# GpSimd additions that wait for the VectorE sum ahead of them in a list schedule

## The chip, the core and the metric

The kernel runs on one core of a Trainium2 chip. The core has five engines that run side by side, each with its own in-order queue: TensorE (PE, with its weight loads shown as PEld), VectorE (DVE), ScalarE (ACT), GpSimd (POOL) and SyncE (SP, which here only issues DMAs). The metric is the device time of one execution in microseconds (us); three runs of the kernel as it was took 1032.78, 1033.08 and 1033.87 us, the median is 1033.08.

## The reference

Linear attention with exponential features, then a mixture of experts with Sinkhorn routing. Cut to what is computed (shapes of this case in comments):

```python
def phi(x):                                   # q, k, v: 8 x 8 x 576 x 64, w_phi: 64 x 128
    proj = np.einsum('bhsd,df->bhsf', x, w_phi)
    proj = proj - np.max(np.abs(proj), axis=-1, keepdims=True)
    return np.concatenate([np.exp(proj), np.exp(-proj)], axis=-1)
q_p, k_p = (phi(q), phi(k))
kv = np.einsum('bhsf,bhsd->bhfd', k_p, v)
...
x = attn_out.transpose(0, 2, 1, 3).reshape(B * S, H * D)      # 4608 x 512
P = np.exp(x @ w_gate - logits.max())                          # 4608 x 8 experts
for _ in range(8):
    P /= P.sum(1, keepdims=True) + 1e-09
    P /= P.sum(0, keepdims=True) + 1e-09
    P *= N / E
for e in range(E):
    h = np.maximum(x @ w1[e], 0.0)            # w1: 8 x 512 x 1024
    out += P[:, e:e + 1] * (h @ w2[e])        # w2: 8 x 1024 x 512
```

Every token goes through every expert, so the eight pairs of matrix products are most of the work.

## The kernel before

**Stages.** From 0 to about 202 us the attention runs, batch by batch, with expert 0's products filled in between. Then come the routing (`routing`) and experts 1 to 7. The tokens are cut into nine groups of 512 (`g`); groups 0 to 7 are taken in pairs, group 8 (the rests of all batches) alone. Per expert there are thus nine steps, two for each pair and one for group 8; the whole of an expert takes about 111 us in the profile.

**Seven products.** Experts 1 to 7 multiply 2 x 2 blocks with seven block products in place of eight (the Strassen-Winograd scheme), which needs sums and differences of blocks in bf16 and additions of results in f32. `up7` makes h = relu(x w1) and `down7` adds P times (h w2) to the result tile `acc` (4 x 512 f32 per group). The sums of blocks come from `sums_x` (of x, kept in DRAM and read back), `sums_up` (of w1), `sums_down` (of w2) and the loop over `fp` in `down7` (of h). All of them go through the helper `sub` (line 1205) and are VectorE `tensor_tensor` instructions of line 1209 with both operands and the result in SBUF. The profile names their tiles `hs` (h), `hx` (a tile that holds the sums and the two V buffers), `T`, `X`, `w` and `wx` (the two weight buffers).

**Who empties a PSUM bank.** There are eight banks of 512 f32. In `up7`, ScalarE copies a bank into another (`move`, line 1376) or into U (`keep`, line 1372) or applies the relu (line 1384), and VectorE adds a bank to U with saturation at 0, written to hs (`add`, line 1379). The products `x3` and `x4` share a bank: PE may start `x4` only when line 1379 has read `x3`. In `down7`, VectorE adds P times a bank to acc (`read`, line 1516), or ScalarE writes P times a bank into V (`read2`, line 1528, two instructions) and GpSimd adds V to acc (line 1531, 128 x 512 f32, both operands in SBUF). There are three such GpSimd additions per group and expert, and two V buffers.

**What sets the order.** Nothing is ordered by hand within a step except the list `ORDER` (line 1581), in which the parts are recorded. Each recorded operation (`Op`) has an engine, an estimated duration and its data dependencies. `Plan.schedule` (line 258) is a list schedule: again and again it takes the operation that can start first by its estimates, ties going to the one recorded first, and appends it to `done`. `Plan.run` (line 316) then issues the instructions in that order; each engine's queue is in order, and instructions of different engines wait for each other only where data requires it. One resource is modelled beside the engines: `Plan.port`, a time until which the operations marked `shared` may not start. VectorE's sums and all GpSimd operations but DMAs are `shared`; the drains of lines 1379 and 1516 are not. In the plan, then, a sum and a GpSimd addition never overlap. On the chip nothing orders them, since they touch different data.

**Other instructions in the queues concerned.** GpSimd's queue also issues the weight loads of the next expert (line 486, two DMAs per expert, behind an addition to group 4's acc). SP's queue reads the x sums back (line 1284) and stores the result (lines 1180 to 1194).

Of the kernel before, what the change touches and what calls it, by code (L numbers as in the profile page):

```python
# [17 lines left out]
class Buf:  # L18


    def __init__(self, ring):
        self.ring, self.t, self.slot, self.left, self.end = ring, None, None, 0, 0.0
        self.last = None
# [91 lines left out]

class Op:
    __slots__ = ("eng", "dur", "lat", "nbytes", "fn", "left", "ready", "users", "idx", "end",
                 "bufs", "deps", "shared", "turn", "unit", "stop", "tiled")

    def after(self, user):  # L120

# [77 lines left out]
class Plan:  # L199
# [3 lines left out]
    def __init__(self):  # L203
        self.last, self.readers = {}, {}
        self.ops = []
        self.prio = 0
        self.port = 0.0

    def op(self, eng, dur, lat, fn, r=(), w=(), takes=(), nbytes=0, shared=False):


        o = Op()
        o.eng, o.dur, o.lat, o.fn, o.nbytes = eng, dur, lat, fn, nbytes
        o.users, o.idx, o.end, o.ready = [], len(self.ops) + self.prio, None, 0.0
        o.shared, o.turn, o.unit, o.tiled = shared, False, 0, 0
        deps = {}
        for key in r:
            for d in self.last.get(key, ()):
                deps[id(d)] = d
        for key in w:  # L220
            for d in list(self.last.get(key, ())) + self.readers.get(key, []):
                deps[id(d)] = d
        bufs = list(takes)
        for key in list(r) + list(w):
            b = key[0] if isinstance(key, tuple) else key
            if isinstance(b, Buf):
                bufs.append(b)
        o.bufs = list({id(b): b for b in bufs}.values())
        for b in o.bufs:
            b.left += 1  # L230
        for key in r:
            self.readers.setdefault(key, []).append(o)
        for key in w:
            self.last[key] = [o]
            self.readers[key] = []
        o.deps = list(deps.values())
        o.left = len(o.deps)
        for d in o.deps:
            d.users.append(o)
        self.ops.append(o)  # L240
        return o

    def start(self, o, free):

        t = max(free, o.ready, self.port if o.shared else 0.0)
        need = {}
        for b in o.bufs:
            if b.slot is None:
                n = need[b.ring] = need.get(b.ring, 0) + 1
                at = b.ring.find(n)  # L250
                if at is None:
                    return None
                t = max(t, at)
            elif b.last is not None and b.last.eng != o.eng:
                t = max(t, b.last.end)
        return t

    def schedule(self):
        ready = {}
        free = {}  # L260
        links, clock = Links(), Clock()
        for o in self.ops:
            if o.left == 0:
                ready.setdefault(o.eng, []).append(o)
        done = []

        def finish(o):
            for b in o.bufs:
                if b.ring.psum:
                    b.last = o  # L270
                b.left -= 1
                b.end = max(b.end, o.end)
                if b.left == 0:
                    b.ring.give(b.end, b.slot)
            for u in o.users:
                u.left -= 1
                u.ready = max(u.ready, o.after(u))
                if u.left == 0:
                    ready.setdefault(u.eng, []).append(u)

        while len(done) < len(self.ops) or links.next():
            best = None
            for eng, rq in ready.items():
                f = free.get(eng, 0.0)
                if best is not None and f > best[0]:
                    continue
                for o in rq:
                    t = self.start(o, f)
                    if t is not None and (best is None or (t, o.idx) < best[:2]):
                        best = (t, o.idx, o)  # L290
            landed = links.next()
            if landed and (best is None or landed[0] <= best[0]):
                o = links.land(*landed)
                o.end = landed[0] + 1.0
                finish(o)
                continue
            assert best is not None, "no operation can start"
            at, _, o = best
            ready[o.eng].remove(o)
            for b in o.bufs:  # L300
                if b.slot is None:
                    b.slot = b.ring.take(at)
            dur = clock.takes(at, o.dur, o.tiled) if o.eng == "PE" else o.dur
            free[o.eng] = at + dur
            if o.shared:
                self.port = at + dur
            done.append(o)
            if o.nbytes:
                links.add(o, at)
            else:  # L310
                o.stop = at + dur
                o.end = o.stop + o.lat
                finish(o)
        return done

    def run(self, tc):
        done = self.schedule()
        with tc.manual_schedule():
            for o in done:
                o.fn()  # L320


@with_exitstack
def kernel(
# [158 lines left out]
    def load_w(e, r=()):  # L483
        w1, w2 = new("w1"), new("w2")
        for w, src in ((w1, moe_w1), (w2, moe_w2)):
            dma("POOL", 2 << 20, 280, lambda w=w, src=src: nc.gpsimd.dma_start(
                out=w(), in_=src[e].rearrange("(c p) f -> p c f", p=128)),
                r, [(w, i, j) for i in range(2) for j in range(2)])
        return w1, w2
# [569 lines left out]
    def stage_g(b):  # L1059
# [4 lines left out]
    at = [0]  # L1064
# [6 lines left out]
    order = (  # L1071
        "lraeaepqbwlqaqawwabwmqlltnrbppnwqbppmrmanbqaqmwwacmpnpbccpwbtcnmqnaqbclupunm"
        "taumquglcapalbcpnqqdcenmucugbblnapmrcqdutabnqpmunpbambccddnqplanmqmducpblttb"
        "augnaqlnrbdcampcadmqeutunqcppmdcaqtdqabpbbmlrqtdnpmuaqualbnagnacctbmqulupran"
        "tdpmtdqcmdnpdabdancpcabbqmpumqbcdgnappqunburqcbugmmnqdcdanumupqbnucmcpnmbddp"
        "bqmpncncubncmmgccg"
    )
# [25 lines left out]
    o = plan.op("X", 0.0, 0.0, swap, w=["late"])  # L1103
# [201 lines left out]
    def load_x(gs):  # L1305
        X = new_x()
        for n in (2, 3, 4):
            move_x(gs, n, False, X)
        return X
# [269 lines left out]


    ORDER = "X1 x10 w10 x11 X2 x20 y10 x21 Z1 y11 X3 w11 x30 x31 x40 x41 w20 Y1 w21 X4 Z2".split()
    END = "X1 p2 Y1 X2 Z1 p3 X3 Z2 X4 p0 p1".split()
    slots, wait = list(range(6)), []

    def take():
        z = [new(f"H{n}") for n in sorted(slots[:2])]
        del slots[:2]
        return z
# [16 lines left out]
    for e in range(1, E):  # L1605
        w1, w2 = load_w(e, ["late", ("acc", 4, 0, 0)] if e > 1 else ["late"])
        if e == 1:
            nextX = sums_x(pairs[0])
        A7 = sums_up(e, w1)
        B7 = sums_down(e, w2) if e > 1 else None  # L1610
        turn = [*pairs, (8,)] if e < E - 1 else [(8,), *pairs]
        for n, gs in enumerate(turn):
            X = nextX if e == 1 else load_x(gs)
            H = {g: [] for g in gs}
            for fp in range(len(gs)):
                hs = take()
                for i, z in enumerate(hs):
                    H[gs[min(i, len(gs) - 1)]].append(z)
                un = up7(A7, gs, fp, X, H, ["up0"])
                for o in ORDER:  # L1620
                    if len(o) == 3:
                        un[o[:2], int(o[2])]()
                    elif dn is not None:
                        dn[o]()
                if dn is not None:
                    dn["out"]()
                    slots.extend(dn["slots"])
                if e == 1 and fp == 0 and n + 1 < len(turn):
                    nextX = sums_x(turn[n + 1], [(H[gs[0]][0], 0, 1, 1)])
                if B7 is None and fp:  # L1630
                    B7 = sums_down(e, w2)
                if fp == len(gs) - 1:
                    wait += [(e, g, H[g], B7, w2, [z.ring.number for z in H[g]]) for g in gs]
                dn = next_down()
    last = next_down()
    for o in END:
        (dn if o[0] in "XYZ" else last)[o]()
# [32 lines left out]
```

## Time and profile before

| | |
|---|---|
| runs | 1032.78, 1033.08, 1033.87 us |
| the profiled execution's own time | 1032.32 us |
| its span, first to last instruction | 1030.2 us |
| PE busy | 1008.4 us (98%), 7944 matmuls |
| VectorE busy | 786.1 us (76%), 1707 instructions |
| ScalarE busy | 745.0 us (72%), 1594 |
| GpSimd busy | 380.0 us (37%), 418 |
| GpSimd additions, line 1531 | 186, 236.2 us in all, 1262 / 1268 / 1426 ns (min, median, max) |
| VectorE sums of 512 columns, `hx<-hx,hs` of line 1209 | 124, 409 / 416 / 1449 ns |
| VectorE sums of 1024 columns, `hx<-w` of line 1209 | 6, 691 / 1201 / 1722 ns |
| drains of line 1379 | 252, 673 / 690 / 694 ns |
| granted TensorE clock | 1.00 |

How to read it: the span is one profiled execution; the time of a run has about 2 us around it. Busy time is recorded time, and matmuls overlap in it: one of 256 columns is recorded with 0.27 us while the next starts 0.11 us later. The profile names instructions by line, engine, operation and tiles (out<-in), and puts idle time down to the instruction whose semaphore ended it. A line can be a helper's: all sums are line 1209, the products of the experts are lines 1317 and 1326. In a timeline, like instructions that follow each other are merged into one row with their number (x2) and their time from the first start to the last end.

### The profile page before, as it was taken

What the parts mean: (1) busy time and instruction counts of PE and PEld (TensorE: products, weight loads), DVE (VectorE), ACT (ScalarE), POOL (GpSimd) and SP (SyncE); (2) the same over time, 40 slices, a digit from 0 to 9 for tenths busy, and PEclk for the clock granted to TensorE, in tenths of its full rate; (3) what the DMA queues carried; (4) which work ended last, traced back from release to release, by engine and by line L of the source; (5) the groups of instructions that cost most, each with busy time, mean ns of one, the idle gap of its engine ahead of it and who ended that gap; (6) DMA issues with size and microseconds to landing.
All of it is one profiled execution on the core that took longest, in us unless ns stands there. A gap on an engine that the chain in (4) does not pass through costs nothing.

```text
span 1030.2 us, 21214 instructions
## 1 busy us (share of the span) xinstructions
PE 1008.4 (98%) x7944; PEld 685.3 (67%) x7944; DVE 786.1 (76%) x1707; ACT 745.0 (72%) x1594; POOL 380.0 (37%) x418
## 2 busy tenths in 40 slices
PE   7899999999999999999999999999999999999998
PEld 5666666644666766676667666676667666776665
DVE  8999989986877776677677766777667766877765
ACT  7999999747888766666666666666666666666663
POOL 5778764400133222322233323322233333323222
PEclk9999999999999999999999999999999999999999
DMA  9999998150104201261116111510125111512333
GB/s 249 195 191 182 167 143 122 37 109 21 41 31 80 60 31 32 41 120 31 32 27 113 37 37 37 89 46 31 31 54 106 32 32 26 109 42 72 124 126 130
DMA packets 107014, 82.84 MB, mean 80 GB/s; under 512 B 53536, under 2 KB 89376, under 8 KB 106912
## 3 DMA queue, kind: packets, MB, share of 16 engines
q1 hardware_dynamic: 74960, 57.44, 22.6%
q0 software_dynamic: 31648, 23.86, 17.0%
q8 instruction: 62, 1.02, 0.4%
q14 instruction: 40, 0.33, 0.1%
q10 hardware_dynamic: 304, 0.20, 0.1%
HBM read 83.18 MB, written 12.98 MB: 93 GB/s over the span
## 4 chain that ended last, share of the span: by engine, by line
PE 92%; DVE 3%; ACT 2%; issue 2%; DMA 1%; SPq 0%; DVEq 0%; ACTq 0%
PE ps L1317 41%; PE ps L1326 31%; PE ps L591 18%; PE ps L874 2%; DVE hs L1379 1%; DMA acc<-in_q_dram 1%; ACT k L587 1%; ACT q L587 1%; DVE m L583 0%; DVE wx L583 0%; PE ps L721 0%; PE ps L903 0%; ACT kr L587 0%; ACT wx L587 0%; DVE ps L882 0%
## 5 line engine op out<-in xcount | busy, mean ns | idle before, releaser
L1531 POOL TENSOR_TENSOR acc<-acc,hx 128x512 f32<-128x512 f32 x186 | 236.2, 1270 | 573.1 <-ACT hx L1528 569.2
L1317 PEld LDWEIGHTS <-hs 128*128 128x128 bf16 x1984 | 194.1, 98 | 71.8 <-issue 0.9
L1516 DVE SCALAR_TENSOR_TENSOR acc<-ps,P,acc 128x256 f32<-128x256 f32 x372 | 163.5, 479 | 94.9 <-PE ps L1317 85.9
L1379 DVE CUSTOM_DVE_ANT_0 hs<-ps,U 128x512 bf16<-128x512 f32 x252 | 169.4, 686 | 51.9 <-PE ps L1326 35.3
L1376 ACT COPY ps<-ps 128x512 f32<-128x512 f32 x252 | 144.0, 587 | 77.9 <-PE ps L1326 65.9
L1384 ACT ACTIVATE hs<-ps 128x512 bf16<-128x512 f32 x252 | 151.5, 605 | 54.4 <-PE ps L1326 48.0
L1528 ACT ACTIVATE hx<-ps,P 128x256 f32<-128x256 f32 x372 | 156.3, 473 | 46.4 <-PE ps L1317 44.9
L1317 PEld LDWEIGHTS <-hx 128*128 128x128 bf16 x1488 | 145.6, 98 | 38.7
L1326 PE MATMUL ps<-X,T 128*128 128x512 bf16 x448 | 132.8, 379 | 0.0
L1317 PE MATMUL ps<-hx,hs 128*128 128x256 bf16 x992 | 129.0, 273 | 0.6 <-ACT hx L1528 0.6
L1326 PE MATMUL ps<-xT,wx 128*128 128x512 bf16 x384 | 105.2, 379 | 0.0
L1326 PEld LDWEIGHTS <-T 128*128 128x128 bf16 x672 | 65.8, 98 | 51.8
L1209 DVE TENSOR_TENSOR hx<-hs 128x512 bf16<-128x512 bf16 x124 | 50.4, 420 | 42.6 <-PE ps L1317 27.3
L1326 PE MATMUL ps<-xT,w 128*128 128x512 bf16 x288 | 78.8, 379 | 0.0
L1372 ACT COPY U<-ps 128x512 f32<-128x512 f32 x126 | 74.7, 593 | 4.0 <-PE ps L1326 3.9
L1547 ACT COPY ps<-ps 128x512 f32<-128x512 f32 x62 | 35.7, 575 | 57.8 <-PE ps L1317 45.0
L1326 PEld LDWEIGHTS <-wx 128*128 128x128 bf16 x512 | 50.1, 98 | 41.1 <-issue 3.9
L1317 PE MATMUL ps<-wx,hs 128*128 128x256 bf16 x560 | 75.8, 273 | 0.0
L1326 PE MATMUL ps<-xT,T 128*128 128x512 bf16 x224 | 74.9, 379 | 0.0
L591 PE MATMUL ps<-xT,w 128*128 128x512 bf16 x288 | 72.9, 379 | 0.0
L591 PE MATMUL ps<-w,hx 128*128 128x512 bf16 x288 | 72.8, 379 | 0.0
L1317 PE MATMUL ps<-wx,hx 128*128 128x256 bf16 x496 | 67.7, 273 | 0.0
(149 smaller groups left out, 1660.3 us busy)
## 6 DMA issues: line engine op xcount, KB each, us to landing
X<-xd SPq DMA_DIRECT2D x72, 256.0 KB, 2.7
wx<-in_moe_w_dram POOLq DMA_DIRECT2D x8, 1024.0 KB, 12.3
v_m<-in_v_dram SPq DMA_DIRECT2D x15, 512.0 KB, 5.6
out_dram<-acc SPq DMA_DIRECT2D x14, 512.0 KB, 2.7
w<-in_moe_w_dram POOLq DMA_DIRECT2D x6, 1024.0 KB, 11.9
qk<-in_k_dram POOLq DMA_DIRECT2D x12, 256.0 KB, 5.5
qk<-in_q_dram POOLq DMA_DIRECT2D x12, 256.0 KB, 6.4
xd<-X SPq DMA_DIRECT2D x12, 256.0 KB, 2.0
```

What stands on the lines that cost most here:

```text
L591: nc.tensor.matmul(out_, lhsT=lhsT, rhs=rhs, start=start, stop=stop)
L1209: lambda: f.tensor_tensor(out=out_(), in0=x(), in1=y(), op=op), r, w, **kw)
L1317: pe(256, lambda i=i, k=k, z=z: nc.tensor.matmul(bank()[:, 256 * i:256 * i + 256], lhsT=lhs(k, i), rhs=rhs(k), start=first and z, stop=k = ...
L1326: pe(512, lambda k=k: nc.tensor.matmul(bank().rearrange("p (a b) -> p a b", a=2), lhsT=lhs(k), rhs=rhs(k), start=first and k == 0, stop=k ...
L1372: act(512, lambda: nc.scalar.copy(out=u[q]().rearrange("p a b -> p (a b)"), in_=w[q]()), [w[q]], [u[q]])
L1376: act(512, lambda: nc.scalar.copy(out=to[q](), in_=x[q]()), [x[q]], [to[q]])
L1379: dve(515, lambda: nc.vector._custom_dve(ADD_SAT, out=out_(q, i, j), in0=bank[q]().rearrange("p (a b) -> p a b", a=2), in1=u[q](), s0=3.0e ...
L1384: act(512, lambda: nc.scalar.activation(out=out_(q, i, j), in_=bank[q]().rearrange("p (a b) -> p a b", a=2), func=ACT.Relu, bias=0.0, scal ...
L1516: dve(320, lambda n=n, ts=ts: nc.vector.scalar_tensor_tensor(out=acc[g][:, ts, 256 * j:256 * j + 256], in0=bank()[:, 256 * n:256 * n + 256 ...
L1528: act(370, lambda n=n: nc.scalar.activation(out=u()[:, n, :], in_=bank()[:, 256 * n:256 * n + 256], func=ACT.Copy, bias=0.0, scale=P[:, 4 ...
L1531: pool(695, lambda: nc.gpsimd.tensor_tensor(out=acc[g][:, 2 * i:2 * i + 2, 256 * j:256 * j + 256], in0=acc[g][:, 2 * i:2 * i + 2, 256 * j: ...
L1547: act(512, lambda: nc.scalar.copy(out=y(), in_=x()), [x], [y])
```

## The change

`Plan` remembers the last VectorE operation that was marked `shared` (`self.vector`). Two things follow from it. In `start`, a `shared` GpSimd operation may begin, by the plan's estimates, only at that operation's `end`, which is 0.15 us after its `stop`; before, only the port's being free counted. And where it is planned to begin less than 1.5 us after that stop, it keeps the VectorE operation as `behind`; `run` then adds a dependency, so that on the chip the GpSimd instruction waits for a semaphore of that VectorE instruction. The estimates, and hence the order in which operations are taken, are those of the same list schedule. `EARLY` holds the same list as `ORDER`, so the last two parts of the diff change nothing. Line numbers in the changed file are 12 to 15 higher from line 324 on: 1209 becomes 1221, 1379 becomes 1391, 1516 becomes 1528, 1531 becomes 1543.

```diff
--- before.py
+++ after.py
@@ -115,7 +115,7 @@
 
 class Op:
     __slots__ = ("eng", "dur", "lat", "nbytes", "fn", "left", "ready", "users", "idx", "end",
-                 "bufs", "deps", "shared", "turn", "unit", "stop", "tiled")
+                 "bufs", "deps", "shared", "turn", "unit", "stop", "tiled", "ins", "behind")
 
     def after(self, user):
 
@@ -204,7 +204,7 @@
         self.last, self.readers = {}, {}
         self.ops = []
         self.prio = 0
-        self.port = 0.0
+        self.port, self.vector = 0.0, None
 
     def op(self, eng, dur, lat, fn, r=(), w=(), takes=(), nbytes=0, shared=False):
 
@@ -213,6 +213,7 @@
         o.eng, o.dur, o.lat, o.fn, o.nbytes = eng, dur, lat, fn, nbytes
         o.users, o.idx, o.end, o.ready = [], len(self.ops) + self.prio, None, 0.0
         o.shared, o.turn, o.unit, o.tiled = shared, False, 0, 0
+        o.ins = o.behind = None
         deps = {}
         for key in r:
             for d in self.last.get(key, ()):
@@ -243,6 +244,8 @@
     def start(self, o, free):
 
         t = max(free, o.ready, self.port if o.shared else 0.0)
+        if o.eng == "POOL" and o.shared and self.vector:
+            t = max(t, self.vector.end)
         need = {}
         for b in o.bufs:
             if b.slot is None:
@@ -304,6 +307,10 @@
             free[o.eng] = at + dur
             if o.shared:
                 self.port = at + dur
+                if o.eng == "DVE":
+                    self.vector = o
+                elif self.vector and at < self.vector.stop + 1.5:
+                    o.behind = self.vector
             done.append(o)
             if o.nbytes:
                 links.add(o, at)
@@ -317,7 +324,12 @@
         done = self.schedule()
         with tc.manual_schedule():
             for o in done:
-                o.fn()
+                o.ins = o.fn()
+                if o.behind:
+                    tc.add_manual_dep(
+                        o.ins.ins, o.behind.ins.ins.name, mybir.DependencyInfo(
+                            mybir.DependencyClass.Sync, mybir.DependencyReason.DATA),
+                        reason="order at the shared port")
 
 
 @with_exitstack
@@ -1579,6 +1591,7 @@
 
 
     ORDER = "X1 x10 w10 x11 X2 x20 y10 x21 Z1 y11 X3 w11 x30 x31 x40 x41 w20 Y1 w21 X4 Z2".split()
+    EARLY = ("X1 x10 w10 x11 X2 x20 y10 x21 Z1 y11 X3 w11 x30 x31 x40 x41 w20 Y1 w21 X4 Z2").split()
     END = "X1 p2 Y1 X2 Z1 p3 X3 Z2 X4 p0 p1".split()
     slots, wait = list(range(6)), []
 
@@ -1617,7 +1630,7 @@
                 for i, z in enumerate(hs):
                     H[gs[min(i, len(gs) - 1)]].append(z)
                 un = up7(A7, gs, fp, X, H, ["up0"])
-                for o in ORDER:
+                for o in EARLY if e == 1 else ORDER:
                     if len(o) == 3:
                         un[o[:2], int(o[2])]()
                     elif dn is not None:
```

## The prediction

> **What bounds the kernel now.** I read the page's busy times first, then the busy times by stage, then the waits of each engine, and last the timeline of single instructions around the longest waits. TensorE (PE) is busy for 98% of the span. By stage (the windows view; columns are window, length, then busy time and count of PE, PE weight loads, VectorE, ScalarE, GpSimd, the granted clock, DMA share, GB/s):
>
> ```profile
> 0.00:202.00 202.00, 192.15 (x2217) 128.35 (x2218) 184.99 (x423) 189.26 (x463) 132.26 (x218) 1.00 1.02 163
> 202.00:1012.00 810.00, 801.61 (x5622) 546.38 (x5620) 591.64 (x1265) 552.38 (x1125) 242.68 (x196) 1.00 0.25 58
> 1012.00:1030.30 18.30, 14.64 (x111) 10.55 (x109) 9.52 (x21) 3.35 (x8) 5.07 (x4) 0.98 0.45 173
> ```
>
> The change acts in the second stage. There PE is idle for 810.00 - 801.61 = 8.4 us of 810, at a granted clock of 1.00, so nothing but those 8.4 us (and what hides beside them, below) can be won. The waits of PE name nearly all of it:
>
> ```profile
> engine line waited for: us in total, times, longest us
> PE ps L1326 <- DVE hs L1379: 7.8, 10, 0.8
> ...
> PE ps L1317 <- ACT hx L1528: 0.6, 1, 0.6
> ```
>
> So ten times PE waited for a VectorE instruction of line 1379, the saturating addition that empties a bank into hs, and once (at 273 us) for ScalarE; 7.8 + 0.6 = 8.4. What made VectorE late is in the timelines of VectorE, GpSimd and PE, here around the two waits of one expert (start, length, engine, line):
>
> ```profile
> 575.42 0.42 DVE L1209 TENSOR_TENSOR hs<-hs 128x512 bf16<-128x512 bf16 x1
> 576.80 0.69 DVE L1379 CUSTOM_DVE_ANT_0 hs<-ps,U 128x512 bf16<-128x512 f32 x1 [0.96 <-PE ps L1326]
> 577.41 1.44 DVE L1209 TENSOR_TENSOR hx<-hx,hs 128x512 bf16<-128x512 bf16 x1
> 578.78 1.27 DVE L1379 CUSTOM_DVE_ANT_0 hs<-ps,U 128x512 bf16<-128x512 f32 x2
> ...
> 590.41 1.72 DVE L1209 TENSOR_TENSOR hx<-w 128x1024 bf16<-128x1024 bf16 x1
> 592.05 1.27 DVE L1379 CUSTOM_DVE_ANT_0 hs<-ps,U 128x512 bf16<-128x512 f32 x2
> ```
>
> ```profile
> 575.94 2.63 POOL L1531 TENSOR_TENSOR acc<-acc,hx 128x512 f32<-128x512 f32 x2 [6.12 <-ACT hx L1528]
> ...
> 588.94 2.64 POOL L1531 TENSOR_TENSOR acc<-acc,hx 128x512 f32<-128x512 f32 x2 [6.12 <-ACT hx L1528]
> ```
>
> ```profile
> 591.23 0.71 PE L1317 MATMUL ps<-wx,hs 128*128 128x256 bf16 x5
> 592.78 0.59 PE L1326 MATMUL ps<-X,w 128*128 128x512 bf16 x2 [0.85 <-DVE hs L1379]
> ```
>
> The reader should see this order of events. GpSimd makes two additions one after the other (2.63 us, 1.27 each); the second begins at 577.30 (its end at 578.57 less 1.27), a VectorE sum begins at 577.41 and lasts 1.44 us where its kind has a median of 0.416. It ends at 578.85, just after the addition. The drain of line 1379 behind it in VectorE's queue is late by that much, and PE, whose next product goes into the same bank, stands. The second place is the same with a sum of 1024 columns: the addition holds from 590.31 to 591.58, the sum takes 1.72 instead of 0.69, PE stands until 592.78. Both engines' operands lie in SBUF; whichever comes 0.1 us later waits.
>
> **What the change removes.** PE's matmuls of 256 columns start (0.71 - 0.27)/4 = 0.11 us apart though each is recorded with 0.27, so every wait hides another 0.27 - 0.11 = 0.16 us: the ten cost 7.8 + 10 x 0.164 = **9.4 us**. Place by place: four of the first kind (355.8, 467.2, 578.6, 800.5 us) at 0.85, six of the second (368.9, 480.3, 591.7, 702.2, 813.6, 924.3) at 1.01; 3.4 + 6.0 = 9.4. Does the change reach them? I compared the built instruction order of the two kernels. At the second place the order is unchanged (sum, then second addition), and that addition now waits for exactly that sum: sum 590.41 to 591.10, drain 591.10 instead of 592.05, its end at 591.78; PE is due there at 591.23 + 5 x 0.11 = 591.78. At the first place the list schedule, which now lets an addition start only 0.15 after the sum ahead of it, puts the sum and two more (those that ran at 579.98 and 580.31) ahead of the drain of 576.80, and both additions wait for the third. So all ten should go; the wait at 273 us, worth 0.58 + 0.16 = 0.74, stands in expert 1, whose order is rearranged from 267 to 312 us, and is open.
>
> **What it adds and moves.** 134 of the 186 additions of line 1531 get a wait on VectorE beside the one on ScalarE; the built program has 105 more separate semaphore waits in GpSimd's queue. Such a wait takes 17 to 43 ns there; 105 x 0.02 = 2 us in 810 on an engine that is busy for 243. Behind a waiting addition stand the next additions and, once per expert, the two weight loads of line 486; ScalarE waits for an addition when it needs one of the two V buffers again. Additions come in twos, then one, then 6.12 us idle; an addition later by 0.7 to 1.3 us is covered by that idle time. Taken: 0; expert 1, where the twos are rearranged, has its own bound below. Matmul count, DMAs, and the order of SP are unchanged; the first 202 us and the last drains and stores are as before.
>
> The real price is in VectorE's order: sums now stand in longer runs ahead of drains of line 1379 that PE waits for. Three kinds of places:
> (a) the four first places: three sums from 575.76, 0.33 to 0.45 apart by the neighbouring rows, end the run so that the drain starts between 576.77 and 577.1 against 576.80 now. PE has some 0.05 to spare. So 0 to 0.3 each, 0 to 1.2 in all; I take 0.1 each, 0.4, as most starts in these rows are 0.34 apart.
> (b) thirteen places, twice per expert, where a sum lasts about 0.95 behind an addition already now without PE standing (651.33 is one). One more sum goes ahead of the drain:
>
> ```profile
> 651.33 0.95 DVE L1209 TENSOR_TENSOR hs<-hs 128x512 bf16<-128x512 bf16 x1
> 652.20 0.41 DVE L1209 TENSOR_TENSOR hx<-hx,hs 128x512 bf16<-128x512 bf16 x1
> 653.12 1.29 DVE L1379 CUSTOM_DVE_ANT_0 hs<-ps,U 128x512 bf16<-128x512 f32 x2 [0.50 <-ACT U L1372]
> ```
>
> That drain waited 0.50 for U from ScalarE, and this hides the sum's 0.34 plus the 0.1 by which the addition now starts later. Taken: 0; with 0.45 for the sum and 0.2 for the lag it is 0.15 each, 2.0 in all.
> (c) expert 1 and the single-group step of each expert (557 to 569), where much PE order changes too: between -0.74 (the wait of 273 us goes) and +2.5 (two additions' length); taken 0, since in both stretches PE stood at most once before.
> (d) the weight loads of six experts, issued when the addition ahead of them ends (656.28 after 655.07 + 1.27). The addition comes some 0.2 later, and the loads with it. By the tile view they land 9.3 and 15.0 us after issue, at 665.6 and 672.1; the sums that read them start at 665.99 and 672.57. The cover is 0.4 and 0.5 here, none at 561.18. Taken: 0; at most 0.2 each, 1.2.
>
> In the Trainium skill, "VectorE: DVE Perf Modes", section "The DRAIN you can't avoid", has a rule against this change: after an operation the pipe empties for about its duration less 266 ns before the next begins. By that estimate a sum would take 0.42 + 0.15 = 0.57, the run in (a) would be 0.7 longer, and some 2.6 us would be given back, for about 1026.3. The rows disagree (sums at 588.24 and 588.58 start 0.34 apart), and I go by the rows.
>
> **Sum.** The profiled execution took 1032.32 us (span 1030.2, and 2.1 around it): 1032.32 - 9.4 + 0.4 = 1023.3. The median of the runs is 1033.08, 0.76 above it, so **1024.0 us**. With the bounds: 1033.08 - 9.4 - 0.74 = 1022.9 to 1033.08 - 9.4 + 1.2 + 2.0 + 2.5 + 1.2 = 1030.6.
>
> **Rivals.**
> 1. *Half the gain.* The six second places go, the four first ones do not: there the fix rests on a changed order, not on the wait alone, and if the run of sums holds the drain as long as the addition did, only 6.0 is won: 1027.0. With the costs of (b) and (c) it reaches 1030.9. For it: PE has 0.05 to spare. Against it: three sums are 1.0, the lost time there was 1.03 beyond the sum itself, and the run starts 1.6 earlier.
> 2. *Slower, by the same queue.* VectorE is in order, so a sum put ahead of a drain that PE waits for is a stall. There are 4 + 6 + 13 = 23 such places; the change breaks even at 9.4/23 = 0.41 each and is slower by 0.2% (2.1 us) at 0.50. If the sums put ahead wait for their own inputs (VectorE waited 14.8 us in 19 waits of 0.8 for relu outputs of line 1384) and lose 0.6 each, it takes 1033.08 - 9.4 + 13.8 = 1037.5. Against it: the 0.50 of cover at (b), and at the second places nothing is moved ahead.
> 3. *No effect.* If the long sums come from something other than the addition (a slow operand), they stay: 1033.1. Against it: at all ten places the sum ends 0.28 (512 columns) or 0.55 (1024) after an addition's end.
>
> **Chances.** The measurement tells about 0.2%, 2 us, from no change. Forecast (1022.4 to 1025.6) 0.60; rival 1 and like sums of costs (1025.6 to 1031.0) 0.23; rival 3 or a cancelling 0.06; rival 2 0.09; below 1022.4, 0.02. Faster 0.60 + 0.23 + 0.02 = 0.85. The range goes from 1022.4 (the lower bound, less the 0.5 by which runs of one kernel differ here) to 1030.5, just under the upper bound, with somewhat over 0.8 in it.
>
> **What would show it.** The row "PE ps <- DVE hs" of PE's waits falls from ten to none or a few; no 512-column sum of 1.4 and no 1024-column sum of 1.7 is left; sums of 0.95 at (b) stay; PE's idle time from 202 us to the end of the stage falls from 8.4 to under 1.5; GpSimd's busy time stays near 380. Wrong would be: a new wait of PE for line 1379 at (a) or (b) places, a wait of ScalarE (V buffers) for GpSimd, or the stage as long as before with the long sums gone.

## The result and the profile after

The changed kernel takes 1022.03 us (median of four runs, 1021.83 to 1023.53) where the kernel before takes 1032.93 (four runs, 1031.85 to 1033.87): a ratio of 0.9898, 95% interval 0.9881 to 0.9915. The mechanism was the one forecast, and the gain was 2 us larger: 1024.0 was predicted, and 1022.03 lies 0.4 below the lower end of the range.

The profiled execution took 1022.21 us, its span 1020.4. The stages of the changed kernel, in the columns of before (window, length, busy time and count of PE, PE weight loads, VectorE, ScalarE, GpSimd, clock, DMA share, GB/s):

```profile
0.00:202.00 202.00, 191.73 (x2212) 128.59 (x2213) 184.70 (x422) 188.97 (x462) 132.19 (x218) 1.00 0.98 163
202.00:1002.00 800.00, 800.00 (x5624) 546.49 (x5622) 583.06 (x1266) 551.03 (x1124) 242.18 (x196) 1.00 0.25 58
1002.00:1020.50 18.50, 14.84 (x113) 10.72 (x110) 9.72 (x21) 3.54 (x9) 5.08 (x4) 0.99 0.44 171
```

The second stage is about 10 us shorter and has the same work; PE shows no idle time in it. The other two are as they were. The waits of PE by cause in the changed kernel begin so:

```profile
engine line waited for: us in total, times, longest us
PE ps L733 <- DMA acc<-in_k_dram: 4.4, 1, 4.4
PE ps L603 <- DVE wx L595: 0.7, 3, 0.3
```

The row that stood first before, hs from the drain (7.8 us, ten times), is gone, and so is the 0.6 for ScalarE's hx at 273 us. What is left is in attention.

The same expert as in the prediction, VectorE first: this is the run of sums that now stands ahead of the drain at the first place (the first place lies 3.85 us earlier here, because the waits before it are gone).

```profile
571.58 0.42 DVE L1221 TENSOR_TENSOR hs<-hs 128x512 bf16<-128x512 bf16 x1
571.91 0.42 DVE L1221 TENSOR_TENSOR hx<-hx,hs 128x512 bf16<-128x512 bf16 x1
572.24 0.42 DVE L1221 TENSOR_TENSOR hs<-hs 128x512 bf16<-128x512 bf16 x1
572.58 0.42 DVE L1221 TENSOR_TENSOR hx<-hx,hs 128x512 bf16<-128x512 bf16 x1
572.95 0.69 DVE L1391 CUSTOM_DVE_ANT_0 hs<-ps,U 128x512 bf16<-128x512 f32 x1
...
585.72 0.68 DVE L1221 TENSOR_TENSOR hx<-w 128x1024 bf16<-128x1024 bf16 x1
586.32 1.28 DVE L1391 CUSTOM_DVE_ANT_0 hs<-ps,U 128x512 bf16<-128x512 f32 x2
```

GpSimd in the same stretch of the changed kernel, with the idle time before each row and what ended it:

```profile
573.43 2.61 POOL L1543 TENSOR_TENSOR acc<-acc,hx 128x512 f32<-128x512 f32 x2 [6.76 <-ACT hx L1540]
...
584.46 1.27 POOL L1543 TENSOR_TENSOR acc<-acc,hx 128x512 f32<-128x512 f32 x1 [6.33 <-DVE hx L1221]
586.57 1.27 POOL L1543 TENSOR_TENSOR acc<-acc,hx 128x512 f32<-128x512 f32 x1 [0.84 <-DVE hx L1221]
```

Read the two together. At the first place the last of the sums is over at 573.00, before GpSimd begins at 573.43, and none is stretched. (Here ScalarE's hx came last, by the row; at the first place of the expert before, GpSimd's row at 463.66 says "<-DVE hx L1221", 0.14 after the last sum's end.) At the second place the wide sum takes 0.68 (1.72 before) and ends at 586.40; the second addition, which used to follow the first at once, has now waited 0.84 us "<-DVE hx L1221" and begins 0.17 us after the sum's end. The drain follows the sum at 586.32, and PE does not stand.

Long sums in the trace of the second stage and the end, by their length:

| | before | after |
|---|---|---|
| 512 columns, 1.4 us or more | 4 | 1 (at 276.4, no wait of PE) |
| 1024 columns, 1.7 us | 6 | 0 |
| 1024 columns, about 1.0 us | 5 | 0 |
| 512 columns, 0.93 to 1.01 us before, 1.05 to 1.18 after | 16 | 14 |

### The profile page after: what moved, and what is told of

Its sections match the earlier page's. It is cut to its first block, busy times and chain, and to the rows that moved or that the text cites. A ratio compares the mean times of both kernels' runs of the same rounds, so it can differ in the third digit from the quotient of the medians.

```text
span 1020.4 us, 21307 instructions
## 1 busy us (share of the span) xinstructions
PE 1006.6 (99%) x7944; PEld 685.8 (67%) x7944; DVE 777.5 (76%) x1707; ACT 743.5 (73%) x1594; POOL 379.5 (37%) x418
## 4 chain that ended last, share of the span: by engine, by line
PE 95%; DVE 2%; ACT 1%; DMA 1%; issue 0%; POOL 0%; SPq 0%; DVEq 0%; POOLq 0%
PE ps L1329 41%; PE ps L1338 33%; PE ps L603 18%; PE ps L886 2%; DMA v_m<-in_v_dram 1%; ACT q L599 0%; PE ps L733 0%; DVE m L595 0%; DMA acc<-in_k_dram 0%; DVE wx L595 0%; PE ps L915 0%; ACT k L599 0%; ACT wx L599 0%; POOL wx L791 0%; DVE ps L894 0%
## 5 line engine op out<-in xcount | busy, mean ns | idle before, releaser
L1396 ACT ACTIVATE hs<-ps 128x512 bf16<-128x512 f32 x252 | 151.0, 604 | 43.0 <-PE ps L1338 34.8
L1221 DVE TENSOR_TENSOR hx<-hs 128x512 bf16<-128x512 bf16 x124 | 50.9, 421 | 46.7 <-PE ps L1329 34.6
## 6 DMA issues: line engine op xcount, KB each, us to landing
wx<-in_moe_w_dram POOLq DMA_DIRECT2D x8, 1024.0 KB, 12.4
w<-in_moe_w_dram POOLq DMA_DIRECT2D x6, 1024.0 KB, 12.0
```

Of the source, the lines that this page charges most:

```text
L1221: lambda: f.tensor_tensor(out=out_(), in0=x(), in1=y(), op=op), r, w, **kw)
L1396: act(512, lambda: nc.scalar.activation(out=out_(q, i, j), in_=bank[q]().rearrange("p (a b) -> p a b", a=2), func=ACT.Relu, bias=0.0, scal ...
```

## The experiments

In each, the times in brackets are the lowest and highest run, and the kernel before was run on the same chip (its median is given). Line numbers shift with the edit: the sums are line 1219 and the drain 1389 in the first four kernels and in the narrow one, 1209 and 1379 in those made from the kernel before.

**The wait alone.** The changed kernel with the order of before:

```diff
     def start(self, o, free):
         t = max(free, o.ready, self.port if o.shared else 0.0)
-        if o.eng == "POOL" and o.shared and self.vector:
-            t = max(t, self.vector.end)
```

> The order of before, with the waits: the list schedule may start an addition where it did before, but each addition planned within 1.5 us of a sum waits for that sum. Theory (the port: an addition that starts 0.1 us ahead of the sum holds it up): all ten waits of PE for the drain of line 1379 go, 9.4 us, the wait of ScalarE's place at 273 us stays; about 1023.5 against 1032.9, no 512-column sum of 1.4 and no 1024-column sum of 1.7 us left. Rival (the new order does it, the waits are not needed): no gain, 1033. Rival (half the gain): only the six places with a sum of 1024 columns go, 1027.

Measured: 1022.95 (1022.76 to 1023.74) against 1032.51, ratio 0.9906 [0.9889, 0.9922]. All ten waits are gone; of PE's waits in the experts only the one for ScalarE's hx is left (0.6, at 274 us). So the semaphores alone bring nearly everything, at the first places too, and the rearranged runs of sums are not needed for it.

**The order alone.** The other half: the rearranged list, no semaphores.

```diff
                 if o.eng == "DVE":
                     self.vector = o
-                elif self.vector and at < self.vector.stop + 1.5:
-                    o.behind = self.vector
```

> The order of the changed kernel without one wait. Theory (the port): the six second places lose their 1.0 us as before, since the addition again starts ahead of the sum, and at the four first places the additions start inside the longer run of sums and hold up the drain by one addition or more; 1031 to 1039. Rival (the order does it): 1022, like the changed kernel. If the order settles the first places alone: 1028.

Measured: 1040.94 (1040.3 to 1042.66) against 1032.51, ratio 1.0083 [1.0068, 1.0098]: 8.4 us slower, more than any theory had. The waits of PE in this kernel:

```profile
PE ps L1336 <- DVE hs L1389: 11.6, 11, 1.7
...
PE ps L1327 <- DVE acc L1526: 2.7, 5, 0.5
PE ps L1327 <- DVE hs L1389: 1.7, 1, 1.7
```

They add up to 16.0, 8.2 more than the 7.8 of before, close to the loss of 8.4. What happens at a first place, VectorE and then GpSimd:

```profile
580.64 1.49 DVE L1219 TENSOR_TENSOR hs<-hs 128x512 bf16<-128x512 bf16 x1
582.05 1.48 DVE L1219 TENSOR_TENSOR hx<-hx,hs 128x512 bf16<-128x512 bf16 x1
583.46 1.87 DVE L1389 CUSTOM_DVE_ANT_0 hs<-ps,U 128x512 bf16<-128x512 f32 x3
```

```profile
580.49 2.77 POOL L1541 TENSOR_TENSOR acc<-acc,hx 128x512 f32<-128x512 f32 x2 [5.42 <-ACT hx L1538]
```

Nothing but its own input holds GpSimd back, so it begins in the middle of the run of sums, and now two sums run into two additions: each takes 1.48 instead of 0.42, and PE stands 1.69 at 584.19. The theory was short by this second sum, and by five waits for the drain of line 1526 that no theory had. These have the same cause: five sums `hx<-w,hx` or `hx<-wx,hx` of 1024 columns, each just ahead of that drain, take 1.75 to 1.76 us. One begins at 600.55, 0.19 after an addition (600.36, 1.39 long); the drain follows at 602.23, and PE has stood 0.53 when it goes on at 603.14. In the changed kernel the addition waits for that sum, which takes 0.69 there (589.41). The plan's order is worth something only with the semaphore that enforces it.

**The wait only for wide sums.** The wait alone, kept only where the sum ahead has 1024 columns:

```diff
-                elif self.vector and at < self.vector.stop + 1.5:
+                elif self.vector and self.vector.dur > 0.5 and at < self.vector.stop + 1.5:
```

> The order of before, with the waits only where the sum ahead is one of 1024 columns. Theory: the six second places go at 1.0 us each, the four first ones stay: 6.0 us, about 1026.9, and PE's waits for the drain fall from ten to four of about 0.7 recorded. Rival (the gain is spread over all additions, or comes from somewhere else): not 6 us but a share by the number of waits, under 2 us.

Measured: 1026.82 (1026.28 to 1027.62) against 1032.51, ratio 0.9944 [0.9929, 0.9959], 5.7 us faster. The six second places are gone; five waits of PE for hs, 3.4 us, remain: the four first places and a new one at 687 us (on which more below, with the kernel before run again).

**The wait for an older sum.** The control: GpSimd gets as many semaphores, but each for the sum before the one that matters, which has mostly long ended (VectorE ends 26 of GpSimd's waits for its input in this trace, ScalarE 125; in the changed kernel VectorE ends 93). The order is that of before, as in the wait alone.

```diff
                 if o.eng == "DVE":
-                    self.vector = o
+                    self.older, self.vector = self.vector, o
                 elif self.vector and at < self.vector.stop + 1.5:
-                    o.behind = self.vector
+                    o.behind = self.older
```

> The order of before, and as many waits, each for the sum before the one that stands ahead, which is long done. It has the price of the wait as an instruction without holding the addition back. Theory: 1033, ten waits of PE as before, and no price that can be measured (GpSimd is idle for most of the time). Rival (the extra semaphore instruction itself delays the addition enough): a gain of several us, towards 1023.

Measured: 1033.05 (ten runs, 1032.28 to 1035.06) against 1032.51, ratio 1.0009 [1.0, 1.0019]. PE's waits are those of before and one more:

```profile
PE ps L1336 <- DVE hs L1389: 8.4, 11, 0.8
```

GpSimd's queue has 180 separate semaphore entries for the additions here (173 in the changed kernel, 68 before), and they neither help nor cost more than the interval tells. So it is not the number of semaphores that helps, but which sum an addition waits for.

**The changed kernel and the wait alone once more**, both unedited, on one chip:

> The changed kernel again, beside the waits alone (next run) on the same chip. Theory: the waits give 9.4 us and the new order about 1 more (the wait at 273 us, 0.65, and six hidden ones of 0.065 behind the sums T<-w,T); about 1022.0. Rival: the order gives nothing, both at 1022.5 within 0.3.

> The order of before with the waits, a second time. Theory: 1.0 us above the changed kernel, 1023.0. Rival: equal to it within 0.3.

Measured on one chip, against 1032.44: the changed kernel 1021.81 (1021.3 to 1022.41), ratio 0.9897 [0.9882, 0.9911]; the wait alone 1023.63 (1022.97 to 1025.23), ratio 0.9916 [0.9902, 0.9931]. The new order is worth 1.8 us here; by the first runs of the two, which were not measured side by side, it is 0.9 by the medians and 1.3 by the gains. The two intervals of the ratios overlap, but the runs of this pair do not, and the direction is the same both times. The profiled executions of this pair lie 2.24 us apart. By the starts of the same matmuls, 1.17 of that arises before expert 1, where PE's order is the same in both kernels (two executions of the kernel before differ by 1.1 there); 1.07 arises in the experts: 0.70 in expert 1, 0.37 at six short waits (both below).

**Additions half as long.** In the kernel before, every GpSimd addition does half its columns; the other half of the result is left out.

```diff
-                out=acc[g][:, 2 * i:2 * i + 2, 256 * j:256 * j + 256],
-                in0=acc[g][:, 2 * i:2 * i + 2, 256 * j:256 * j + 256], in1=u(), op=ALU.add),
+                out=acc[g][:, 2 * i:2 * i + 2, 256 * j:256 * j + 128],
+                in0=acc[g][:, 2 * i:2 * i + 2, 256 * j:256 * j + 128],
+                in1=u()[:, :, 0:128], op=ALU.add),
```

> Before, without any wait, each GpSimd addition cut to half its columns; it leaves the other half of these additions out. The addition takes some 0.67 us in place of 1.27 by its columns. Theory (the sum waits for the addition's end): each wait of PE shrinks by the 0.6 to 0.66 us by which the addition ends earlier, from 0.85 to 0.2 at the four or five first places and from 1.0 to 0.35 at the six second ones; 6.3 to 7 us less than before, about 1026. Rival (a sum that meets an addition pays a fixed price, or its own operands are slow): ten or eleven waits of the same length, 1032.5.

Measured: 1026.82 (1026.44 to 1027.54) against 1032.44, ratio 0.9947 [0.9931, 0.9964]. An addition of 256 columns takes 0.73 us (median 726 ns), not the 0.67 taken. The sums of the two places in this kernel, and the additions they ran into:

```profile
574.84 0.90 DVE L1209 TENSOR_TENSOR hx<-hx,hs 128x512 bf16<-128x512 bf16 x1
...
587.29 1.17 DVE L1209 TENSOR_TENSOR hx<-w 128x1024 bf16<-128x1024 bf16 x1
```

```profile
574.73 0.72 POOL L1531 TENSOR_TENSOR acc<-acc,hx 128x256 f32<-128x256 f32 x1 [0.64 <-ACT hx L1528]
...
587.19 0.72 POOL L1531 TENSOR_TENSOR acc<-acc,hx 128x256 f32<-128x256 f32 x1 [0.64 <-ACT hx L1528]
```

The additions end at 575.45 and 587.91, the sums at 575.74 and 588.46: 0.29 and 0.55 later, as with whole additions (0.28 and 0.55). The sum's length goes with what is left of the addition; a fixed price per meeting falls. PE's waits for hs shrink from 7.8 us in ten to 1.8 in six; the four first places still wait 0.14 each, which is under the 0.15 from which the view counts. So each of the ten is 0.54 to 0.55 shorter (0.69 to 0.14, 0.84 to 0.30), as the addition is.

**Additions twice as long.** The changed kernel, with a second GpSimd operation of the same size, whose result nobody uses, behind each addition:

```diff
-            pool(695, lambda: nc.gpsimd.tensor_tensor(
+            pool(695, lambda: (nc.gpsimd.tensor_tensor(
...
+                nc.gpsimd.tensor_tensor(out=u(), in0=u(), in1=u(), op=ALU.add))[0],
```

> The changed kernel, waits and order, with a second addition of the same size on GpSimd straight after each one (V added to itself, which nothing reads). It asks how much room the waits leave. Theory: the waits order an addition only against the sum ahead of it, and the sum that follows it is held until both end, 1.27 us later; at the second places (six) and at the thirteen places with a sum of 1.17 us, PE comes to wait about 1 us each, the V buffers come free later beside; slower than before, 1040 to 1065, with PE waiting for line 1391 some twenty times or more. Rival (with the waits the port is settled and GpSimd's length no longer matters, as it is idle for 60% of the time): 1022 to 1024.

Measured: 1056.56 (two runs, 1056.28 and 1056.84), ratio 1.0233 [1.0213, 1.0254] to the kernel before, 34.8 over the changed one on the same chip (1021.81). The size is in the range of the theory, the place is not: PE waits

```profile
PE ps L1338 <- DVE acc L1528: 9.3, 40, 0.6
PE ps L1338 <- DVE hs L1391: 9.0, 19, 0.8
...
PE ps L1329 <- DVE acc L1528: 3.5, 6, 0.9
```

mostly for the other drain (line 1528), which other sums hold up; the wide sum of the second place still got in ahead of the added operation. The semaphore orders an addition behind the sum ahead of it. It does nothing for the sums that come while GpSimd runs; these are safe only as long as the addition is short.

**The kernel before, twice more**, to see whether it is chance which places stand:

> Before, profiled a second time. In the first profile the sum at 689 us was not held up, while the same place in every other expert was; two experiments in the order of before showed five first places, not four. Theory (a race of 0.1 us decides who holds the other up, so one execution differs from the next): ten or eleven waits of PE for line 1379, four or five first places, six second ones. Rival (the number is fixed by the order): exactly the ten of the first profile, at the same places.

> Before, a third time: the same question. Theory: ten or eleven waits, with the place at 689 us the one that changes, and 0.85 us between such executions. Rival: ten, at the same places.

Measured: 1033.42 and 1032.38 us (spans 1031.3 and 1030.3), and in both traces the same ten waits at the same places, 7.8 us. The rival was right for this kernel: its places are fixed, not drawn anew each time. Why does the expert at 689 us escape at its first place? In the kernel before, VectorE and GpSimd there:

```profile
688.81 0.41 DVE L1209 TENSOR_TENSOR hx<-hx,hs 128x512 bf16<-128x512 bf16 x1
```

```profile
687.34 1.26 POOL L1531 TENSOR_TENSOR acc<-acc,hx 128x512 f32<-128x512 f32 x1 [6.12 <-ACT hx L1528]
688.99 1.36 POOL L1531 TENSOR_TENSOR acc<-acc,hx 128x512 f32<-128x512 f32 x1 [0.39 <-POOL acc L1531]
```

The second addition starts 0.39 after the first one's end, and so 0.18 after the sum's start. The view names the first addition as what it waited for, but that wait stands at the other first places too, and there the second starts 0.10 after the first; what holds it 0.29 longer at 689 us no run shows (it is there in all three profiles of the kernel before). The sum takes 0.41, the addition 1.36 instead of 1.27, and PE does not stand. What follows is the change in small: here the addition comes second and loses 0.09, for which nobody waits; at the other first places the sum comes second and loses 1.03, for which PE waits.

The same place in the kernel with waits for wide sums, whose order is the same, GpSimd and then VectorE:

```profile
684.52 2.64 POOL L1541 TENSOR_TENSOR acc<-acc,hx 128x512 f32<-128x512 f32 x2 [6.12 <-ACT hx L1538]
685.99 1.45 DVE L1219 TENSOR_TENSOR hx<-hx,hs 128x512 bf16<-128x512 bf16 x1
```

Here the second addition starts 0.10 after the first (at 685.89), 0.10 ahead of the sum, and the sum is held; with waits for older sums it is the same (690.94 and 691.05). This is the new wait of PE in both kernels. So the places are fixed by the program, but not by the order alone.

**The wait only for narrow sums.** The mirror of the wide one, `self.vector.dur < 0.5`, also in the order of before:

```diff
-                elif self.vector and at < self.vector.stop + 1.5:
+                elif self.vector and self.vector.dur < 0.5 and at < self.vector.stop + 1.5:
```

> The order of before, with the waits only where the sum ahead has 512 columns (the other half of the run with the waits at 1024 columns, which won 5.7 us). Theory: the four or five first places go at 0.85 us, the six second ones stay: 3.4 to 4.3 us, about 1028.5, and the two halves add up to what all the waits gave (9.2). Rival (the halves are not independent, a first place that goes makes the next one worse): less than 2.5 or more than 5 us.

Measured: 1024.93 (1023.85 to 1025.32) against 1033.03, ratio 0.9918 [0.9902, 0.9935]: 8.1 us faster, twice what the theory of independent halves had. One wait of 0.9 for hs is left, at 917 us. The trace shows why the second places went too, though no addition waits for a wide sum; GpSimd and VectorE at one of them:

```profile
585.84 3.08 POOL L1541 TENSOR_TENSOR acc<-acc,hx 128x512 f32<-128x512 f32 x2 [6.33 <-DVE hx L1219]
```

```profile
585.28 0.42 DVE L1219 TENSOR_TENSOR hx<-hx,hs 128x512 bf16<-128x512 bf16 x1
...
587.11 0.68 DVE L1219 TENSOR_TENSOR hx<-w 128x1024 bf16<-128x1024 bf16 x1
```

The first addition of the pair now waits for the narrow sum that ends at 585.70 and begins at 585.84. It ends at 587.11, and the wide sum begins just then, 0.08 ahead of the second addition (587.19 in the trace), which is now the one that is held: 1.73 us, where the median is 1.27. In the kernel before, the second addition was ahead by 0.10 (590.31 to 590.41). A shift of 0.1 to 0.2 us on either engine decides a stall of 1.0. That is why the halves do not add up: 5.7 + 8.1 = 13.8, where both together in the same order, the wait alone, bring 9.6 and 8.8. That the shift does it is read from this trace, and from the place at 689 us, where a start 0.3 earlier makes the stall; it was not tried by itself.

No version beat the changed kernel. Between 202 and 1002 us PE shows no idle time any more.

## Where the prediction was right, and where it fell short

**What bounds it, and what goes** (9.4 us): right. Comparing the starts of the two profiled executions matmul by matmul, the four first places give 0.85 each, the six second places 1.005 each: 3.4 + 6.0 = 9.4. The cause, an addition that begins 0.1 ahead of a sum, is shown three ways: by ordering the two (the wait alone), by the length of the addition (half as long), and by the control, in which as many semaphores for the wrong sum bring nothing. Rival 3, no effect, is refuted.

**The hidden 0.16 of each wait:** right for the ten, but the same rule was not followed to its end. A wait that is shorter than 0.16 us shows as no idle time at all. There are six such places (455.1, 566.5, 677.9, 788.4, 899.8, 910.9 us in the kernel before), where PE waited about 0.06 for a drain behind three sums; the new order moves those sums, and 0.37 us comes back in all. This term was missing.

**(a) the run of three sums ahead of the drain,** taken as 0.4: it is 0. The drain at 572.95 is exactly the 576.80 of before less 3.85, the time that PE had won by then. The sums' rows show the pace of 0.33 to 0.34 on which this rests. The estimate that the prediction drew from "VectorE: DVE Perf Modes" in the Trainium skill, section "The DRAIN you can't avoid", would have put them 0.57 apart and given back 2.6 us. The same paragraph of that section says that a next operation that is not held starts earlier; the prediction left this out, and the rows, 0.33 to 0.34 apart, agree with the page when it is read with it.

**(b) thirteen places with a longer sum,** taken as 0: right. In the changed kernel, VectorE at the place shown before (647 us here):

```profile
645.63 1.17 DVE L1221 TENSOR_TENSOR hs<-hs 128x512 bf16<-128x512 bf16 x1
...
647.41 0.69 DVE L1391 CUSTOM_DVE_ANT_0 hs<-ps,U 128x512 bf16<-128x512 f32 x1
```

The sum got 0.22 longer (0.95 before) and one more stands behind it, but the drain begins where it did (653.12 less the 5.70 won by then is 647.42). The cover named, 0.50 of waiting for U, was there.

**(c) expert 1,** taken as 0 between -0.74 and +2.5: it is -0.70 (the same matmuls start 0.67 later than in the profile of before at 270 us, and 0.03 earlier at 318). The wait for ScalarE at 273 us goes with the new order and stays (0.6) in every kernel with the old one. The bound held; the value was taken at nothing, though the only wait that the trace showed in this stretch lies in the part that is rearranged.

**(d) the weight loads,** taken as 0: no wait of PE behind them appeared. The addition ahead of them begins at 649.68 where it began at 655.07, 5.39 earlier when PE had won 5.70: 0.3 later than PE, not 0.2, and covered all the same.

**The step that failed is the sum, and with it the lower end of the range.** Three terms were off to one side: (a) was put at 0.4 and is 0; (c) was put at nothing and is -0.70; the hidden waits, 0.37, had no term. Together that is 1.47. The sum itself, 1033.08 - 9.4 + 0.4, is 1024.08 where the prediction writes 1024.0, so it was 2.05 high. The other 0.58 is no effect of the change but the level of single executions: the profiled execution of before lay 0.76 under its median, that of after 0.18 over it (0.94 together); against that the matmuls at the end of the attention came 0.67 later in the profiled execution of after, and 1.8 instead of 2.1 us lay around its span. 0.94 - 0.67 + 0.3 = 0.57, within rounding. The lower end, 1022.4, was the best of all cases less 0.5, with no room for a wait that the view of waits cannot show, and with 0.5 for a spread of medians from runs that differ by up to 2 us (1031.85 to 1033.87). With 0.37 and 1.0 in their place it would have been 1021.6.

**Rival 1, half the gain,** is what the wait for wide sums alone gives: 1026.82 where 1027.0 was worked out, with four of its five remaining waits at the first places. It did not come true because the first places go by the wait (the wait alone keeps the old order and loses none); the new order without it makes them worse. **Rival 2, slower by the queue,** is what the order alone gives, 1040.94 where it had 1037.5; but not because sums ahead of a drain wait for their inputs: they are caught by GpSimd, and the semaphores take this away.

**The tests named:** the row of ten went to none; PE's idle time in the stage from 8.4 to 0; GpSimd's busy time stayed (379.5); the long sums at (b) stayed. One sum of 1.44 is left, at 276.4 us in expert 1, and PE does not wait there.

Open: what holds the second addition 0.29 longer at 689 us in the kernel before, and whether the 1.07 us between the wait alone and the changed kernel that the traces show in the experts is all that the new order brings.

## What to carry to other kernels

When an engine's instruction has a median of 0.42 us and a longest of 1.45, lay its timeline beside that of the engine it may share a path with, and see which of the two began first and how much time the loser costs the bound. If the bound waits for the one and not for the other, fix the order with a semaphore on the side that can afford to come second; a better planned order without the semaphore can be worse than none. And put into the range what the view of waits cannot show (here six waits of 0.06 us), and the scatter of the runs as they lie.

## What the runs showed of the hardware

- The one that begins second, of a sum and an addition, ends when the other has ended, plus its own length, less 0.14 us. Sums behind an addition end 0.28 (0.42 alone) and 0.55 (0.69 alone) after its end, whether the addition takes 1.27 or 0.73. Additions behind a sum follow the same line: at 688.99 of the kernel before, 0.23 of the sum were left and the addition lost 0.23 - 0.14 = 0.09 (1.36); at 587.19 of the kernel with waits for narrow sums, 0.60 were left and it lost 0.46 (1.73). All 31 sums that are held in the kernel before follow it within 0.01 us. So neither side is favoured; the sum loses more because the addition is longer. What the 0.14 is was not tried.
- From the end of a sum to the start of the addition that waits for it pass 0.14 to 0.17 us (585.70 to 585.84 with waits for narrow sums; 586.40 to 586.57 in the changed kernel).
- A hundred more semaphore waits in GpSimd's queue (180 entries for 68, with the wait for an older sum) leave the time at 1.0009 [1.0, 1.0019] of before, one more wait of PE of 0.7 us included.
- An addition of 128x512 f32 takes 1.27 us, one of 128x256 0.73: half the work takes 0.57 of the time.
